# Gated linear attention with a bilinear FFN on one core: block 3's output projection in seven quarter-block products, and a new order of steps

## The chip, the cores and the metric

The kernel runs on one core of a Trainium2 chip. The metric is device time in microseconds (us): the median of several executions. The profile is of one execution; its span (first to last recorded activity) is a little shorter than that execution's own time.

Engines by the profile's names: PE (TensorE, matmuls; PEld are its weight loads), DVE (VectorE), ACT (ScalarE), POOL (GpSimd), SP (SyncE, here only an issuer of DMAs).

## What is computed

Inputs q, k, v and alpha have the shape (4 batches, 8 heads, 768 tokens, 48). Each head keeps a 48 x 48 state; the result of the attention is the FFN's input.

```python
for t in range(S):
    state = alpha[:, :, t, :, None] * state + np.einsum('bhd,bhe->bhde', k[:, :, t], v[:, :, t])
    y[:, :, t] = np.einsum('bhd,bhde->bhe', q[:, :, t], state)
x = y.transpose(0, 2, 1, 3).reshape(B * S, H * D)       # 3072 x 384
out = ((x @ w_a) * (x @ w_b)) @ w_out                   # 384 -> 1536 -> 384
```

Inputs and output are float32; the kernel multiplies in bf16.

## The kernel before, in words

**Blocks.** The 3072 tokens are worked in six blocks (`chunks` 0 to 5), two batches by 256 tokens each: 512 columns, or four groups of 128 rows. Blocks 0 and 1 hold the first 256 tokens of the four batches, 2 and 3 the next, 4 and 5 the last, so the states go from block 0 to 2 to 4 and from 1 to 3 to 5.

**Steps.** The whole kernel is a list, `PROGRAM` (line 17 on). Each entry is `block: step arguments`, and `OPS` maps a step to a function. The program is walked once, and each step puts its instructions behind those already there on its engine; every engine runs its own in that order, and the framework adds the semaphores between engines. So the order of this list sets the order of work on each engine, and a step that has to wait holds up whatever stands behind it on that engine. Engines are named by a letter: V DVE, S ACT, P POOL, Y SP.

*Attention steps.* `ld` loads one of alpha, q, k, v (POOL or SP issues it). `ln`, `l2`, `l2s`, `R`, `AQ`, `ra`, `lv`, `E`, `mk`, `mq` form the decays and put them on keys and queries; `lv` is one DVE or POOL multiplication on half a block of q or k (`level`, L610), `R` a DVE subtraction (`rest`, L581), `E` and `ra` are ACT exponentials. `dr` and `dl` bring the decay of a half block round through DRAM (SP). `T` is a DMA transpose of one batch's keys and queries (SP, L705), `Tr` its rearrangement. `v` and `vs` bring v into two layouts (ACT, DVE or POOL). `K`, `K2` are the state products on PE (L752, L765), with raw v as one operand; `k` is the state's update on DVE (L782, L783). `D` are scores on PE (L797), `M` their masking on DVE, or `Mc` an ACT copy followed by `Mm`, a masking in place on DVE (L814). `SB`, `SA`, `Y` sum the outputs on PE (L826): carried part, then inner part, the latter reading the masked scores. `X` copies the block's transposed output `xT` to SBUF.

*FFN steps.* `a f` and `b f` are one of twelve 128-row gate and up products: three matmuls of 128x512 (L881), or of 128x256 where a block is worked by batch. `as f` copies the gate half to SBUF (ACT), `pr f` multiplies (DVE, L895) into `prod`. `o m h` is half of the output projection for row group m: six matmuls of 128x384 (L903); `ot m` copies the sum out of PSUM, `st m` stores 192 KB.

*Block 4's and 5's output projections* are done otherwise. `w_out` and `prod` are cut in quarters, and seven products of quarter sums stand for the eight plain quarter products. `TW 1` to `4` (DVE, `mix_w`, L960) form mixes of the quarters of `w_out`, once; `S 1` to `4` (DVE, `mix_p`, L971, L974) form mixes of a block's quarters of `prod`, one of them in place. `P n bank` is one quarter product, 12 matmuls of 128x192 (L989), and `P+` adds onto what the bank holds. The result lies in a bank as two halves of 192 columns, for two groups of 128 rows (g = 0 and 1). `z` copies a sum from its bank (L918, L920) or adds an earlier copy to it on DVE (`c11`, `c22`, `c12`, L1001); `zs` stores one quarter of the output (L1007).

**PSUM.** There are eight banks of 512 float32 a partition; the last number of a step is its bank. `wide(i)` is bank i with the next one.

**Buffers.** `prod` has two buffers, so block 5 writes where block 3's was. The mixes live in buffers of the attention inputs: `a_t`, `k_t`, `q_t` (two each) and `la` (one).

**Order around the change.** The list is written out, by blocks of steps from several chunks: while block n is in its FFN, block n+1 is in its attention. Block 3's eight `o` stand among block 5's attention and block 4's first `a` and `b`. Then block 4's and 5's `a`, `b` follow pair by pair, with `TW` and block 4's `S` between them, then block 4's seven products, then block 5's. The last product's sum is copied from one bank in two halves: `z c21 4 S 0` (ACT, g = 0), `z c21 4 V 1` (DVE, g = 1), with one store each from ACT's and SP's queue.

Of the kernel before, what the change touches and what calls it, by code (L numbers as in the profile page):

```python
# [8 lines left out]
F32 = mybir.dt.float32  # L9
# [69 lines left out]
1: C 1 0 2; Ce 1 0 S; v 1 V; vs 1 0 S  # L79
0: o 1 0 0; o 1 1 -; ot 1 S  # L80
1: SA 0; Y 0
2: l2s 0 V
1: K2 1 1 2 1; X 0 S
0: cs 1 0 P
2: l2 0 V
1: D 1 1 6; Mc 1 1
0: o 2 1 -; ot 2 S
1: a 2 0 0; as 2 0; a 4 0 4
2: l2s 1 V
1: b 2 0 5  # L90
2: ra 1; lv 1 q P
1: vs 1 1 V
2: R 0
1: D 1 0 6; as 4 0; k 1 0 V
2: ra 0
1: SB 1 2
2: R 1
1: k 1 1 V
2: AQ 0; E 1 i; ld v * P; E 1 b
1: pr 2 0; a 10 0 4; as 10 0; a 7 0 5; M 1 0; a 1 0 6; Mm 1 1 V; b 4 0 7; pr 4 0; b 1 0 1; a 5 0 4; as 1 0; pr 1 0  # L100
2: lv 0 q P; E 0 b; dr
1: b 10 0 6; pr 10 0; a 6 0 7; as 7 0; b 7 0 1; pr 7 0; b 5 0 5; as 5 0
2: lv 1 k P
1: b 11 0 6; pr 5 0; SA 1
2: mq 0 V
1: Y 1
2: mq 1 V
1: b 6 0 1
2: mk 1 V; E 0 i
1: as 6 0; a 0 0 0; b 0 0 7; pr 6 0; a 11 0 4; X 1 S; a 2 1 5; b 3 0 2; as 0 0; pr 0 0; as 11 0; a 3 0 3; as 3 0; a 8 0 4; b 9 0 0; b 2 1 1; a 6 1 3; pr 11 0  # L110
1: as 2 1; a 9 0 5; as 9 0; pr 3 0; o 2 0 2
3: ln *; l2s 0 P; l2 0 P
0: st 0 Y
1: a 5 1 5; pr 2 1
2: lv 0 k V
1: as 8 0; a 8 1 1; as 8 1; b 8 0 6; a 3 1 7; pr 9 0; a 10 1 0
2: mk 0 V
1: pr 8 0
2: T 1
1: b 8 1 4; pr 8 1; b 5 1 1  # L120
2: dl
1: as 5 1; pr 5 1
3: l2s 1 P
1: as 6 1; b 6 1 6; pr 6 1; as 3 1; b 3 1 3; pr 3 1
2: Tr 1 S; K2 * * 4 5; k * 0 V
1: as 10 1; b 10 1 1; pr 10 1
2: k * 1 V
1: a 9 1 3; as 9 1; o 2 1 -
3: ra 1
2: v 0 S; T 0  # L130
1: b 9 1 3; pr 9 1; a 4 1 0; a 1 1 1
2: v 1 S; vs 1 0 V
1: b 11 1 4; as 1 1; a 7 1 6
4: ld a * Y
1: as 4 1
3: ld q * Y
1: b 1 1 5; pr 1 1; b 4 1 3
3: ra 0
1: pr 4 1; a 11 1 7
2: Tr 0 V; D 1 1 0; M 1 1  # L140
# [84 lines left out]
4: lv 0 k P; E 0 i; E 1 i
3: SA 0
4: mk 0 V
3: Y 0; X 0 S; Y 1
4: ld v * P; v 0 V
3: X 1 S  # L230
2: o 1 0 0; o 1 1 -
3: a 2 * 6; a 1 * 2
4: E 1 b; v 1 V; vs 0 0 V
3: a 9 * 3
2: ot 2 S
4: mk 1 V
3: b 2 * 1; as 2 *; as 9 *
4: vs 1 1 S
3: b 9 * 4; b 5 * 3; a 4 * 5
4: mq 1 V; T 0; Tr 0 S  # L240
3: pr 2 *; a 5 * 1
4: dr
3: a 11 * 6; as 11 *; a 3 * 7
5: l2 0 V
3: pr 9 *
4: T 1
3: b 11 * 4
5: l2s 1 V; R 0; R 1
3: pr 11 *; b 4 * 6
2: ot 1 S  # L250
3: as 4 *; pr 4 *; b 3 * 0
5: ra 0
3: b 1 * 4; as 3 *
5: lv 0 q P
3: pr 3 *; a 6 * 5; as 1 *; pr 1 *
4: dl; D 0 1 6; M 0 1
3: as 5 *; pr 5 *; as 6 *
5: lv 0 k V
4: K * 0 0; k * 0 V
2: st 2 Y  # L260
4: Tr 1 S
5: AQ 1
3: b 6 * 4; pr 6 *
4: vs 1 0 S
1: st 1 Y
5: E 1 i
3: a 8 * 5; as 8 *
5: ld v * P; E 0 b; mq 0 V
2: o 3 0 3; o 3 1 -
4: D 1 1 4  # L270
5: E 0 i; E 1 b; dr
2: ot 3 S
4: SB 0 0; D 0 0 6; M 0 0; Mc 1 1
3: b 8 * 2; pr 8 *
5: mk 0 V; lv 1 q V
3: a 7 * 3; as 7 *; a 0 * 4; as 0 *
5: lv 1 k V
4: Mm 1 1 V; SB 1 6
5: mk 1 V
4: vs 0 1 P; SA 0  # L280
2: st 1 Y
4: D 1 0 2; Mc 1 0; Mm 1 0 V; Y 0
3: b 7 * 4; b 0 * 5; pr 0 *
5: mq 1 V
3: a 10 * 2; as 10 *
2: st 3 Y
5: K * 0 3
4: SA 1; Y 1; X 1 S
3: o 2 0 2; b 10 * 5
4: X 0 V; a 0 * 0; a 6 * 1  # L290
5: v 0 V
3: pr 10 *; pr 7 *
5: T 0; T 1
4: a 3 * 5; b 3 * 4; as 3 *
5: dl
# [12 lines left out]
3: ot 1 V; o 3 1 -
5: D 1 1 2
4: as 6 *  # L310
5: D 0 0 0; Mc 0 0; Mc 1 1
3: ot 3 V
5: D 1 0 6; M 1 0
3: st 2 Y
4: b 6 * 4; pr 6 *
3: o 0 0 5
5: SB 0 0; vs 0 0 V; SB 1 2; D 0 1 6; M 0 1
4: a 7 * 4
5: Mm 0 0 V
3: o 0 1 -; ot 0 V  # L320
5: vs 1 0 S; Mm 1 1 V
3: st 3 Y; st 0 Y
4: a 4 * 6
5: SA 1; SA 0; vs 0 1 S; Y 0; X 0 V; vs 1 1 S; Y 1; X 1 V
3: st 1 Y
4: b 9 * 5; pr 9 *; as 7 *; b 7 * 4; pr 7 *; TW 1 V; as 4 *; b 4 * 7; pr 4 *
4: a 5 * 0; as 5 *; b 5 * 1; pr 5 *
4: TW 2 V
4: a 8 * 2; as 8 *; b 8 * 3; pr 8 *
4: TW 3 V  # L330
4: a 1 * 4; as 1 *; b 1 * 5; pr 1 *
# [12 lines left out]
5: a 9 * 6; as 9 *; b 9 * 7; pr 9 *
4: S 3 V
5: a 10 * 0; as 10 *; b 10 * 1; pr 10 *
5: a 7 * 2; as 7 *; b 7 * 3; pr 7 *
5: a 1 * 4; as 1 *; b 1 * 5; pr 1 *
5: a 0 * 6; as 0 *; b 0 * 7; pr 0 *
5: a 2 * 0; as 2 *; b 2 * 1; pr 2 *  # L350
5: a 8 * 2; as 8 *; b 8 * 3; pr 8 *
4: P 1 6; z p1 1 S; P 2 7; z c11 2 V; zs c11 Y; P+ 6 6; z u2 6 S; P 5 0; z p5 5 S
5: S 1 V
4: P+ 7 6; z c22 7 V; zs c22 Y
5: S 2 V
4: P+ 3 0; z c12 3 V; zs c12 Y; P+ 4 6
5: S 3 V; S 4 V
4: z c21 4 S; zs c21 Y
5: P 1 1; z p1 1 S; P 2 2; z c11 2 V; zs c11 Y; P+ 6 1; z u2 6 S; P 5 3; z p5 5 S; P+ 7 1; z c22 7 V; zs c22 Y; P+ 3 3; z c12 3 V; zs c12 Y; P+ 4 1; z c21 4 S 0; z c21 4 V 1; zs c21 S 0; zs c21 Y 1
"""  # L360


@with_exitstack
def kernel(
# [11 lines left out]
    nc = tc.nc  # L376
# [756 lines left out]
```

## Time and profile before

| | us |
|---|---|
| median of 3 runs | 189.93 |
| lowest, highest | 189.7, 190.2 |
| the profiled execution's own time | 189.66 |
| its span | 187.9 |
| PE busy | 180.7 |
| DVE busy | 149.1 |
| ACT busy | 119.2 |
| POOL busy | 51.7 |
| granted TensorE clock | 1.0 throughout |

Matmuls are pipelined: a row's mean duration of one matmul is longer than the distance from one to the next, so the pace is taken from pieces of the chain (a time and a count) and not from the mean. Idle time of an engine ends with a releaser, inferred from semaphores: "[0.79 <-ACT ot L918]" says that the instruction followed 0.79 us of idleness which ended with ACT's. The window rows give, after the stretch and its length, the busy time of PE, PEld, DVE, ACT and POOL with instruction counts in brackets, the granted clock, the DMA share and GB/s.

### The profile page before, as it was taken

How to read it: one execution, taken by the hardware profiler on the slowest of the kernel's cores; microseconds unless marked ns; L12 is line 12 of the kernel's file. 1: busy time of each engine (PE TensorE's matmuls, PEld its weight loads, DVE VectorE, ACT ScalarE, POOL GpSimd, SP SyncE). 2: the span in 40 equal slices, each digit the busy share in tenths (PEclk: the TensorE clock that was granted, in tenths of full speed). 3: DMA queues.
4: the chain of work that ended last, by engine and by line, in shares of the span. 5: the costliest groups of instructions: out<-in, count | busy, mean ns of one | idle time of the engine just before them, and what ended most of it. 6: DMA issues, size and time to landing. Idle time of an engine off the chain costs nothing.

```text
span 187.9 us, 6287 instructions
## 1 busy us (share of the span) xinstructions
PE 180.7 (96%) x2658; PEld 118.0 (63%) x2673; DVE 149.1 (79%) x267; ACT 119.2 (63%) x225; POOL 51.7 (28%) x74
## 2 busy tenths in 40 slices
PE   7979999999999999999999999999999999999992
PEld 3868885566788876645456645555556444448992
DVE  2587988889979799997898999997487988865641
ACT  4467685678984888796898768942567244443230
POOL 8999573995080510007100006000000000000000
PEclk9999999999999999999999999999999999999999
DMA  5999999999998999999999296989322000000233
GB/s 146 254 224 196 265 236 253 233 249 264 243 223 130 160 236 285 278 254 149 186 245 260 48 161 123 85 115 183 59 85 84 9 0 0 0 0 3 85 130 126
DMA packets 65774, 29.43 MB, mean 157 GB/s; under 512 B 55777, under 2 KB 64113, under 8 KB 65745
## 3 DMA queue, kind: packets, MB, share of 16 engines
q1 hardware_dynamic: 46976, 16.34, 40.9%
q0 software_dynamic: 18624, 12.58, 39.4%
q8 instruction: 21, 0.34, 0.7%
q10 hardware_dynamic: 144, 0.10, 0.2%
q14 instruction: 9, 0.07, 0.1%
HBM read 25.98 MB, written 4.74 MB: 164 GB/s over the span
## 4 chain that ended last, share of the span: by engine, by line
PE 86%; ACT 6%; DMA 3%; issue 2%; POOL 1%; DVE 0%; POOLq 0%
PE psum L881 47%; PE psum L903 16%; PE psum L989 7%; PE psum L826 5%; DMA v_t<-in_v_dram 3%; PE psum L797 3%; ACT vx L918 2%; PE psum L696 2%; PE psum L591 1%; ACT la L514 1%; PE psum L752 1%; PE psum L765 1%; PE psum L658 1%; PE psum L549 1%; PE psum L550 1%
## 5 line engine op out<-in xcount | busy, mean ns | idle before, releaser
L881 PE MATMUL psum<-xT,wa_t 128*128 128x512 bf16 (+1 forms) x264 | 56.5, 336 | 0.5 <-issue 0.2
L881 PE MATMUL psum<-xT,wb_t 128*128 128x512 bf16 (+1 forms) x262 | 56.0, 335 | 0.6 <-issue 0.3
L881 PEld LDWEIGHTS <-wa_t 128*128 128x128 bf16 x270 | 25.8, 98 | 19.9 <-issue 0.5
L881 PEld LDWEIGHTS <-wb_t 128*128 128x128 bf16 x270 | 25.6, 98 | 19.5 <-issue 0.3
L903 PE MATMUL psum<-wo_t,prod 128*128 128x384 bf16 x192 | 34.7, 326 | 0.0
L903 PEld LDWEIGHTS <-prod 128*128 128x128 bf16 x192 | 17.9, 98 | 11.8
L610 POOL TENSOR_TENSOR q_t<-q_t,ra 128x384 f32<-128x384 f32 x6 | 6.1, 1009 | 53.9 <-ACT ra L603 30.9
L918 ACT ACTIVATE ot<-psum 128x384 f32<-128x384 f32 (+1 forms) x20 | 9.7, 485 | 12.1 <-PE psum L989 8.0
L918 ACT ACTIVATE vx<-v_t 32x384 bf16<-32x384 bf16 x26 | 13.5, 521 | 0.5
L810 ACT ACTIVATE m<-psum 128x768 bf16<-128x768 f32 x14 | 11.0, 810 | 3.9 <-PE psum L797 3.9
L636 DVE TENSOR_TENSOR QKp<-q_t,beta 128x768 bf16<-128x768 f32 x10 | 9.5, 954 | 2.8 <-POOL q_t L610 1.7
L514 ACT ACTIVATE la<-a_t 128x1536 f32<-128x1536 f32 (+2 forms) x9 | 9.5, 1055 | 2.9 <-DMA a_t<-in_alpha_dram 2.9
L806 DVE TENSOR_TENSOR m<-psum,mask 128x768 bf16<-128x768 f32 x10 | 9.5, 953 | 0.8 <-PE psum L797 0.6
L636 DVE TENSOR_TENSOR QKp<-k_t,invb 128x768 bf16<-128x768 f32 x10 | 9.5, 954 | 0.3
L826 PE MATMUL psum<-m,vx 64*64 64x128 bf16 (+1 forms) x576 | 8.7, 205 | 0.0
L507 POOL DMA_DIRECT2D v_t<-in_v_dram x8 | 8.5, 1064 | 0.0
L989 PEld LDWEIGHTS <-prod 128*128 128x128 bf16 x96 | 8.0, 98 | 0.2
L1001 DVE TENSOR_TENSOR ot<-psum,ot 128x384 f32<-128x384 f32 x6 | 3.3, 557 | 5.9 <-PE psum L989 5.6
L826 PEld LDWEIGHTS <-vx 64*64 64x64 bf16 x576 | 7.6, 108 | 0.2
L826 PE MATMUL psum<-kqT,Sm 64*64 64x128 bf16 x144 | 7.3, 220 | 0.4 <-DVE Sm L779 0.4
L814 DVE TENSOR_TENSOR m<-m,mask 128x768 bf16<-128x768 bf16 x14 | 7.5, 551 | 0.0
L625 ACT ACTIVATE beta<-psum 128x384 f32<-128x384 f32 x10 | 4.8, 495 | 3.5 <-PE psum L596 3.4
(292 smaller groups left out, 341.2 us busy)
## 6 DMA issues: line engine op xcount, KB each, us to landing
out_dram<-ot SPq DMA_DIRECT2D x23, 192.0 KB, 2.1
q_t<-in_q_dram SPq DMA_DIRECT2D x3, 768.0 KB
k_t<-in_k_dram SPq DMA_DIRECT2D x3, 768.0 KB
a_t<-in_alpha_dram POOLq DMA_DIRECT2D x2, 768.0 KB, 12.1
v_t<-in_v_dram POOLq DMA_DIRECT2D x4, 384.0 KB, 7.5
a_t<-in_alpha_dram SPq DMA_DIRECT2D x2, 768.0 KB
a_t<-in_alpha_dram POOLq DMA_DIRECT2D x3, 384.0 KB, 8.2
k_t<-in_k_dram POOLq DMA_DIRECT2D x3, 384.0 KB, 7.1
```

What stands on the lines that cost most here:

```text
L507: eng.dma_start(out=t[:, us, hs].rearrange("p b h r d -> p (b h) (r d)"), in_=src[ch.b0 + us.start:ch.b0 + us.stop, hs, ch.s * 2 * C:(ch.s ...
L514: nc.scalar.activation(out=ch.la[:, us, hs].rearrange("p b h r d -> p (b h r d)"), in_=ch.a[:, us, hs].rearrange("p b h r d -> p (b h r d) ...
L610: eng.tensor_mul(x, x, by)
L636: eng.tensor_mul(QKp[ch.c % 2][:, u, j, :, hs, :D], src[:, u, hs].rearrange("p h r d -> p r h d"), f)
L806: nc.vector.tensor_mul(m, x, maskn())
L810: nc.scalar.activation(out=m, in_=x, func=AF.Copy)
L814: eng.tensor_mul(m, m, maskn())
L826: nc.tensor.matmul(o, lhsT=lhsT, rhs=rhs, start=(g, c) not in begun, stop=False, skip_group_check=True)
L881: nc.tensor.matmul(p, lhsT=(wa_t, wb_t)[w][:, kk, f * 128:(f + 1) * 128], rhs=ch.xT[:, kk, us, :], start=(kk == 0), stop=(kk == KT - 1))
L903: nc.tensor.matmul(op, lhsT=ch.prod[:, f, at:at + C], rhs=wo_t[:, f, :], start=(f == 0), stop=(f == NFF - 1))
L918: nc.scalar.activation(out=o_, in_=i_, func=AF.Copy)
L989: nc.tensor.matmul(o[:, g], lhsT=A[:, f, g * C:(g + 1) * C], rhs=W[:, f], start=(not more and g == 0 and f == 0), stop=(f == LH - 1), skip ...
```

## The change

Everything from the step after block 0's first `ot` (about 45.5 us into the span) is written in a new order; what stands ahead has only other line breaks.

- Block 3's eight `o`, four `ot` (three DVE, one ACT) and four `st` are replaced by `P 2`, `P 1`, `P 5`, `P+ 6`, `P+ 7`, `P+ 3`, `P+ 4` with `S 1` to `S 4` on DVE, four copies on ACT (`p1`, `p5`, `u2`, `c21`), three adds on DVE (`c11`, `c22`, `c12`) and four `zs`. They stand among block 4's and 5's `a` and `b`.
- The buffers for the mixes are taken when each is needed: `mix_w` takes `a_t` at `TW 1` and `k_t` at `TW 3`, `mix_p` takes `la` at `S 4`.
- Block 5's products 1, 6, 7, 4, which add up in one place, are now `Q`: the half g = 0 lies in bank 1, the half g = 1 in bank 2. The last `z`: DVE g = 0 with a store from SP, ACT g = 1 with a store from ACT.
- Steps of blocks 1 to 5 change places. In particular block 4's products begin among block 5's `a` and `b`, and block 5's first product comes ahead of block 4's last. Block 2's `ld v` is issued by POOL behind `lv 0 q` (before: ahead of it); `lv 1 k` of block 2, last in that group before, now comes earlier; block 5's transposes come earlier; block 4's and 5's v loads stand together.

The number of instructions stays the same for every other step.

```diff
-3: o 2 0 2; b 10 * 5
...
-3: o 1 0 0; o 1 1 -
...
-3: ot 1 V; o 3 1 -
...
+3: P 2 5
+4: a 10 * 7
+5: Mm 1 1 V
+3: S 1 V; S 2 V
...
+4: b 7 * 0; b 2 * 1; pr 4 *; a 2 * 2; as 2 *; b 8 * 3; pr 7 *; TW 2 V; a 5 * 0; as 5 *
+3: S 4 V
+4: b 10 * 2; pr 8 *; as 10 *
+3: P 1 6; z p1 1 S
+4: b 5 * 0
+5: a 11 * 3
+4: pr 2 *; TW 3 V; TW 4 V; b 11 * 1; pr 5 *
+3: P 5 7; z p5 5 S
+4: a 1 * 0
+3: P+ 6 6
+4: pr 10 *
+5: a 2 * 2
+3: S 3 V; z c11 2 V
+4: a 11 * 5
+3: z u2 6 S; P+ 7 6
...
+3: P+ 3 7
+4: as 1 *
+3: z c22 7 V
+5: b 6 * 1; a 9 * 0
+3: P+ 4 6
...
+3: z c12 3 V
```

The last stage, and block 2's steps around its v load and its `Y 1`:

```diff
-5: P 1 1; z p1 1 S; P 2 2; z c11 2 V; zs c11 Y; P+ 6 1; z u2 6 S; P 5 3; z p5 5 S; P+ 7 1; z c22 7 V; zs c22 Y; P+ 3 3; z c12 3 V; zs c12 Y; P+ 4 1; z c21 4 S 0; z c21 4 V 1; zs c21 S 0; zs c21 Y 1
+5: S 4 V; P 2 0; z p1 1 S
...
+5: z c11 2 V; zs c11 Y; Q+ 6 1; P 5 3; z u2 6 S; S 3 V; Q+ 7 1; z p5 5 S; P+ 3 3; z c22 7 V; z c12 3 V; zs c22 Y
+5: zs c12 Y; Q+ 4 1; z c21 4 S 1; zs c21 S 1; z c21 4 V 0; zs c21 Y 0
...
-2: AQ 0; E 1 i; ld v * P; E 1 b
...
+2: ra 0; lv 0 q P
...
+2: mq 0 V; ld v * P
...
+2: SB 1 0; vs 0 1 V; SB 0 2; vs 1 0 V
+1: b 11 1 6
+3: R 0
+2: Mm 0 1 V
+1: o 3 0 4; pr 11 1; o 3 1 -; ot 0 S
+3: lv 0 q V
+2: Mm 1 0 V; Y 1; Mm 0 0 V; SA 1; SA 0
```

The functions:

```diff
     def mix_w(n, eng):
-        if n == 1:
-            x, y = (late(t)[:, :2 * LH * HM].rearrange("p (w f e) -> p w f e", w=2, f=LH) for t in "ak")
-            mix.update({1: x[:, 0], 2: x[:, 1], 3: y[:, 0], 4: y[:, 1]})
+        at = (n - 1) // 2
+        if 2 * at + 1 not in mix:
+            x = late("ak"[at])[:, :2 * LH * HM].rearrange("p (w f e) -> p w f e", w=2, f=LH)
+            mix.update({2 * at + 1: x[:, 0], 2 * at + 2: x[:, 1]})
...
-    def block_mm(ch, n, i, more):
+    def block_mm(ch, n, i, more, apart=False):
...
-        o = bank(i)[:, :2 * HM].rearrange("p (g e) -> p g e", g=2)
+        o = wide(i)[:, :, :HM] if apart else bank(i)[:, :2 * HM].rearrange("p (g e) -> p g e", g=2)
...
+        "Q": lambda x, n, i: block_mm(x, int(n), i, False, True),
+        "Q+": lambda x, n, i: block_mm(x, int(n), i, True, True),
```

More of the change, by code (lines that the diff above doesn't have):

```diff
@@ L101 @@
[L101 to L116, printed above, removed]
@@ L236 @@
+4: mq 1 V
+5: ra 1
+3: a 4 * 1; a 3 * 2; as 3 *; b 3 * 3
 4: mk 1 V
[L237 to L259 removed]
@@ new lines @@
+5: lv 1 q V
+3: a 6 * 2; pr 4 *
+1: st 1 Y
+3: as 5 *; pr 5 *; as 11 *; as 1 *; b 11 * 3; a 2 * 4
+4: vs 0 1 P
+3: b 2 * 6
+5: AQ 0
+3: as 2 *
+4: K * 0 7
+3: pr 11 *
+4: D 0 1 4
+3: as 6 *
+5: E 0 i; E 0 b
+4: vs 0 0 V
+3: a 0 * 2; pr 2 *
+4: Tr 1 S
+3: b 6 * 3; b 1 * 0
+4: M 0 1
+5: mk 0 V
+4: k * 0 V
+5: E 1 b; E 1 i
+2: o 3 0 4
+5: dr
+4: vs 1 1 S
+2: o 3 1 -; ot 3 S
+5: lv 0 q P
+4: D 1 1 5
+3: pr 1 *
+4: D 0 0 0
+3: b 8 * 7
+5: mq 0 V
+3: a 8 * 4; pr 6 *
+4: Mc 1 1
+3: as 8 *
+4: Mm 1 1 V; SB 0 5
```

486 lines of the change are left out of this document (260 added, 226 removed).

## The prediction

> **What bounds the kernel now.** I read the page first, then what TensorE (PE) waits for, then the chain of waits, then the last microseconds of the timeline.
>
> ```profile
> span 187.9 us, 6287 instructions
> PE 180.7 (96%) x2658; PEld 118.0 (63%) x2673; DVE 149.1 (79%) x267; ACT 119.2 (63%) x225; POOL 51.7 (28%) x74
> PEclk9999999999999999999999999999999999999999
> ```
>
> ```profile
> PE psum L532 <- DVE og L432: 1.2, 1, 1.2
> PE psum L797 <- ACT bl L679: 0.6, 1, 0.6
> PE psum L881 <- issue: 0.5, 3, 0.2
> PE psum L826 <- DVE Sm L779: 0.4, 1, 0.4
> PE psum L549 <- ACT la L514: 0.4, 1, 0.4
> ```
>
> PE is busy in 96% of the span at full clock. Its listed waits are 3.1 us (us in total, times, longest); the four behind other engines belong to lines that first run in the first 20 us, which the change leaves alone. So PE's own work is the time, and an edit pays if it shortens that work, or the tail behind it, without making PE wait.
>
> ```profile
> 127.87 1.08 PE psum L903 x6
> ...
> 132.19 2.92 PE psum L903 x18
> ...
> 156.20 10.74 PE psum L881 x49
> ...
> 170.61 13.87 PE psum L989 x168
> ```
>
> These pieces of the chain are PE running back to back. L903 is the plain output projection (`o`): 2.92 us for three steps, 0.973 a step of 6. L989 is the quarter product (`P`): 13.87/14 = 0.991 us for 12 matmuls, 82.6 ns each. The `o` at 127.87 stands ahead of 64x64 attention work and costs 1.08: 0.10 us for turning into that work. No row isolates the way back; I take the same.
>
> ```profile
> 184.51 0.33 ACT L918 ACTIVATE ot<-psum 128x192 f32<-128x192 f32 x1 [2.43 <-PE psum L989]
> 184.87 0.37 ACTq L1007 DMA_DIRECT2D out_dram<-ot  x1
> 184.87 0.36 DVE L920 COPY ot<-psum 128x192 f32<-128x192 f32 x1 [0.79 <-ACT ot L918]
> 185.26 0.34 SPq L1007 DMA_DIRECT2D out_dram<-ot  x1
> ```
>
> At the end the two halves of the last sum leave one bank one after the other: DVE's copy waits for ACT's, and its store is issued 0.39 us after ACT's.
>
> **The change part by part.** *Products (PE).* Removed: 8 `o`, 8 x 0.973 = 7.78 us. Added: 7 products, 7 x 0.991 = 6.94. Sum **-0.84**. A product holds PE for 0.99 us beside any neighbour, so standing among gate and up steps changes nothing here.
>
> A rule of the Trainium skill speaks against this term: "TensorE: Matmul & The Clock Gate", "Back-to-back issue gap", has sustained weight-load-and-matmul pairs at 81 ns for 128 columns and 131 for 512. An estimate on the straight line between them is 89 ns for 192 and 114 for 384, so 84 x 89 - 48 x 114 = +2.0 us. This case's trace disagrees: 82.6 ns and 2.92/18 = 162 ns, and 10.74/49 = 219 for 128x512.
>
> *Order on PE.* The new order leaves the full-array steps for 64x64 work 28 times instead of 27, counted in the program. One more way in and out: **+0.20**.
>
> *Last sum.* In two banks, the DVE half needs only its own six matmuls, which end 6 x 0.083 = 0.5 us before PE does. So its 0.36 us copy and SP's issue are over when ACT's copy ends; the last store is then ACT's, issued 0.39 us before the store that is last now. **-0.36**, a little kept back for the shared queue.
>
> *Added DVE and ACT work.*
>
> ```profile
> L974 DVE TENSOR_TENSOR q_t<-q_t,prod 128x1536 bf16<-128x1536 bf16 x2 | 1.9, 946 | 0.0
> L1001 DVE TENSOR_TENSOR ot<-psum,ot 128x384 f32<-128x384 f32 x6 | 3.3, 557 | 5.9 <-PE psum L989 5.6 <-issue 0.3
> L920 DVE COPY ot<-psum 128x384 f32<-128x384 f32 x4 | 2.2, 556 | 0.8 <-PE psum L903 0.7
> L918 ACT ACTIVATE ot<-psum 128x384 f32<-128x384 f32 x19 | 9.4, 493 | 9.6 <-PE psum L989 5.6 <-DVE ot L1001 2.5 <-PE psum L903 1.5
> ```
>
> ```profile
> 130.00:145.00 15.00, 14.79 (x268) 8.66 (x270) 9.87 (x19) 9.21 (x16) 0.00 (x0) 1.00 0.34 78
> 145.00:158.00 13.00, 12.79 (x82) 5.97 (x73) 11.56 (x18) 4.78 (x8) 0.00 (x0) 1.00 0.06 20
> 158.00:170.60 12.60, 12.55 (x60) 5.77 (x60) 9.49 (x14) 5.97 (x10) 0.00 (x0) 1.00 0.00 1
> ```
>
> DVE gains 4 mixes of 0.946 and 3 adds of 0.557 and loses 3 copies of 0.556: +3.8 us. ACT gains 4 copies for 1: +1.5. By my placing of the new order (steps end to end at the row durations) they fall at 137 to 159 us. The third number after the stretch's length is DVE: 30.9 of 40.6 us. With the addition it is 34.7, 85%, and each mix stands at least one gate or up step ahead of the product that reads it. Cost **0** while that room hides it; uncovered, a mix costs its 0.95. The stores go from 4 of 192 KB to 4 of the same size, and SP issues them in a stretch where DMA is at most 0.34 busy: 0. The lazily taken buffers add no instruction: 0. The four weight mixes keep their length; the first moves ahead to about 129, which relieves the fullest stretch, 145 to 158.
>
> *Reordered steps of blocks 1 to 4.* No row shows a wait that this could remove, so it can only cost. I laid each engine's queue end to end against PE's due times and looked at the thinnest places. Two are late or on the edge.
>
> First, block 2's `Y 1` (due 76.3 us). Behind the copy of block 1's last gate half, DVE has to do in this order a half product, two copies `vs`, `R 0`, a mask product, a half product, block 3's `lv 0 q` and the mask product that `Y 1` reads.
>
> ```profile
> 68.50 0.51 DVE L920 COPY vx<-v_t 32x384 bf16<-32x384 bf16 x2
> ...
> 71.09 0.43 DVE L895 TENSOR_TENSOR prod<-as__1541,psum 128x256 bf16<-128x256 bf16 x1
> 71.42 0.95 DVE L581 TENSOR_TENSOR lh<-l 128x768 f32<-128x768 f32 x1
> ...
> 75.72 0.55 DVE L814 TENSOR_TENSOR m<-m,mask 128x768 bf16<-128x768 bf16 x1
> ```
>
> ```profile
> 123.71 0.55 DVE L610 TENSOR_TENSOR q_t<-q_t,ra 128x384 f32<-128x384 f32 x1
> 124.18 0.55 DVE L610 TENSOR_TENSOR k_t<-k_t,a_t 128x384 f32<-128x384 f32 x1
> ```
>
> ```profile
> 72.00:79.00 7.00, 7.00 (x226) 4.78 (x215) 6.71 (x16) 5.84 (x11) 0.00 (x0) 1.00 1.19 280
> ```
>
> Start to start, a half product is 0.33 (71.09 to 71.42) and an 0.55 operation 0.47 (123.71 to 124.18). So 0.33 + 2 x 0.51 + 0.9 + 0.47 + 0.33 + 0.47 + 0.55 = 4.1 us, begun about 0.5 us after the gate half ends at 71.9: done at 76.5, and 0.1 to 0.2 for the hand-over. Late by 0.15 to 0.35; I take **0.25**. The window says the same of the place: DVE already works 6.71 of 7.00 us there. Behind `Y 1` on PE stand both `SA`, `Y 0` and block 3's sums, and all wait.
>
> Second, block 2's v load, which the state product `K2` reads raw. GpSimd (POOL) now issues it behind `lv 0 q`, and that waits for an exponential late in ACT's queue.
>
> ```profile
> 51.77 1.00 POOL L610 TENSOR_TENSOR q_t<-q_t,ra 128x384 f32<-128x384 f32 x1 [6.74 <-ACT ra L603]
> 52.73 1.19 POOL L507 DMA_DIRECT2D v_t<-in_v_dram  x1
> ```
>
> ```profile
> 64.79 0.63 PE psum L765 x64
> ```
>
> ```profile
> DMA to landing us min/median/max: 5.5/7.5/13.3
> ```
>
> Now it is issued at 52.7, a dozen us ahead of `K2` at 64.8. In the new order ACT reaches the exponential at about 56.4, POOL is through at 57.5, and `K2` is due at 63.8, about 6.3 us later. At the smallest landing, 5.5 us, it is free; at the median, 7.5, it costs 1.2. The range is 0 to 1.2. I take **0.15**, nearest the smallest: no other load is queued by POOL in those microseconds, while several of the eight that make the median were issued in the first stage, behind the weights. In block 4 and 5 POOL issues both v loads together, tens of us ahead of use: 0.
>
> Of SP's queue the loads, decay rows and transposes keep their sequence, and the stores of finished rows move between them.
>
> ```profile
> kqT<-QKp SPq DMA_TRANSPOSE x8, 5.6
> ```
>
> The thinnest is block 3's second transpose, which I place at 90 us: with 5.6 to landing it is there at 95.6, and DVE takes it up at about 96. Cost 0; each us later would cost one. What lies after 130 us has the quiet DMA of the windows above.
>
> *Sum.* -0.84 + 0.20 - 0.36 + 0.25 + 0.15 = **-0.60 us**. Against the profiled execution: 189.66 - 0.60 = 189.06. The median shown is 189.93, 0.27 above it, so I forecast **189.3**.
>
> **The rivals.** *No stall* (both thin places hold): -0.84 + 0.20 - 0.36 = -1.00, so 188.9. For it: my two places are late by less than a hand-over. Against: DVE's 96% in that window.
>
> *v lands at the median.* `K2` waits 1.2 us instead of 0.15: +0.45, so 190.4. For it: the move itself. Against: the quiet queue.
>
> *The last sum gains nothing*, because DVE's half still waits for PE's last matmul or the store queue holds it: -0.24, so 189.7. Against it: separate banks and a wait written for its own matmuls.
>
> *Block 3's q load is late (slower).* DVE's `lv 0 q` stands in front of the mask product of `Y 1`, and DVE reaches it at 75.6 us.
>
> ```profile
> 65.75 2.60 SPq L507 DMA_DIRECT2D q_t<-in_q_dram  x1
> ```
>
> ```profile
> 77.13 0.55 DVE L610 TENSOR_TENSOR q_t<-q_t,ra 128x384 f32<-128x384 f32 x1
> ```
>
> SP issues it at 65.75 now and DVE uses it at 77.13 without a gap, so it landed within 11.4 us; no tighter bound is shown. In the new order SP issues it behind the second transpose, 0.4 us later. If it takes the whole 11.4 it lands at 77.5 and costs 1.9: +1.3, so 191.2. It costs from a landing after 75.6, 9.5 us behind its issue, and turns the change slower than before from 10.1 us. For it: the DMA share of that window is over 1, full. Against it: 280 GB/s there would move the 1.5 MB of this and the load ahead in under 6 us.
>
> *The small products pay their weight load.* If a product among other steps went at the pace of a weight load,
>
> ```profile
> L989 PEld LDWEIGHTS <-prod 128*128 128x128 bf16 x96 | 8.0, 98 | 0.2
> ```
>
> 98 ns for 82.6, 84 of them cost 8.2 us for the 7.78 removed: +1.3 on the sum, 190.6, slower. Against it: 168 in 13.87 us with a load for each.
>
> By the rule of the Trainium skill quoted above, the same term would be +2.0 for -0.84, the time 192.1; the 14 products in the trace speak against it.
>
> **How the numbers follow.** About 0.3% (0.57 us) is what a measurement of this kernel can tell from no change. Chances: forecast (-0.85 to -0.35) 0.42, of which 0.23 beyond 0.57; no stall 0.18; v at the median 0.15, of which 0.04 slower by over 0.57; last sum without gain 0.07; q late 0.16, of which 0.13 slower; weight load 0.02. Faster 0.23 + 0.18 = **0.41**, slower 0.04 + 0.13 + 0.02 = **0.19**, within 0.3% **0.40**. The range starts at the no-stall end with 0.1 for the spread of its terms, **188.8**, and ends at **190.7**, above the late v and the weight load; beyond it lie the upper half of the late q and little else, about 0.1.
>
> **What would show it.** PE's busy time 0.6 to 0.8 us smaller; `P` in 0.99 us pieces among gate and up steps; in the list of PE's waits a DVE mask product before the `Y` of 76 us with 0.15 to 0.35, and possibly a v load before `K2` at 64; the last DVE copy over before ACT's begins, and the span ending about 2.9 us after the last matmul. PE waiting for a mix (DVE, at 145 to 158 us) or for `as` copies would make it wrong, and so would a `q_t` load as releaser of DVE at 75 us.

## The result, and the profile after

The changed kernel takes 192.39 us (median of 6 runs, 191.95 to 192.74) where the kernel before takes 189.88 (6 runs): 1.22% slower, ratio 1.0122, 95% interval 1.0097 to 1.0147. The profiled execution took 192.55 us with a span of 190.8; that of before 189.66 with 187.9. In some runs of the experiments the TensorE clock was granted at 0.83 on average from 10 to 20 us, which makes them about 2 us longer; where the profile of such a run is used below, the text says that PE came late.

The page of the changed kernel, first the span and the busy times:

```profile
span 190.8 us, 6336 instructions
PE 180.9 (95%) x2692; PEld 120.5 (63%) x2709; DVE 155.0 (81%) x271; ACT 120.6 (63%) x228; POOL 53.2 (28%) x74
```

DVE was to gain 3.8 us and gained 5.9. What PE waited for (us in total, times, longest us):

```profile
PE psum L828 <- DMA v_t<-in_v_dram: 1.2, 1, 1.2
...
PE psum L944 <- issue: 0.8, 5, 0.2
PE psum L889 <- issue: 0.5, 1, 0.5
...
PE psum L944 <- DVE m L869: 0.4, 1, 0.4
PE psum L944 <- DVE Sm L842: 0.3, 1, 0.3
```

These waits are new: the v load at `K2`, gate and up steps (L944) waiting for DVE, and 0.5 us in the output sums (L889) that has no releaser. (The short "issue" waits of gate and up steps are not new; they were 0.5 us before.) In PE's timeline of the changed kernel they stand at these places:

```profile
51.65 0.49 PE L944 MATMUL psum<-xT,wb_t 128*128 128x256 bf16 x3 [0.34 <-DVE Sm L842]
54.79 0.49 PE L944 MATMUL psum<-xT,wa_t 128*128 128x256 bf16 x3 [0.35 <-DVE m L869]
66.61 0.69 PE L828 MATMUL psum<-v_t,QKp 64*64 64x48 bf16 x64 [1.20 <-DMA v_t<-in_v_dram]
```

```profile
106.70 0.57 PE L889 MATMUL psum<-m,vx 64*64 64x64 bf16 x36 [0.52 <-issue]
```

The list leaves out the short waits. A finer reading: from 45.5 us on I put PE's steps end to end, each with the duration of its kind (0.648 us for a gate step, 0.976 for `o`, 0.990 for `P` and so on), and take the difference to when each step began. In the kernel before, this lag is 0.1 us at the end. In the changed kernel it comes in four places:

| lag of PE in us at | before | after |
|---|---|---|
| 57 us, block 1's `a 5` | -0.05 | 1.52 |
| block 2's `K2` | -0.03 | 2.80 |
| behind block 2's `Y 1` | 0.0 | 3.09 |
| behind block 3's `Y 0` | 0.11 | 3.79 |
| the last product | 0.13 | 3.85 |

The steps themselves add up to 183.50 us in the new order and 184.18 in the old, so 0.68 less; the lag is 3.72 more; the rest, the stretch behind PE's last matmul, is 0.2 less. That gives +2.8; the two profiled executions differ by 2.9. From 107 us to the end, where the seven products, their mixes and their copies stand, the lag grows by 0.06.

The chain of waits of the changed kernel, around block 3's and block 4's products:

```profile
149.63 0.99 PE psum L1055 x12
150.62 1.94 PE psum L944 x9
152.57 0.99 PE psum L1055 x12
...
176.51 11.07 PE psum L1055 x132
```

A product among gate and up steps takes 0.99 us, as one among products. And the end:

```profile
187.11 0.36 DVE L983 COPY ot<-psum 128x192 f32<-128x192 f32 x1
187.60 0.33 ACT L981 ACTIVATE ot<-psum 128x192 f32<-128x192 f32 x1 [2.48 <-PE psum L1055]
187.96 0.37 ACTq L1073 DMA_DIRECT2D out_dram<-ot  x1
```

DVE's copy is over before ACT's begins, as intended. From the start of ACT's copy to the end of the span it is 190.8 - 187.60 = 3.2 us, before 187.9 - 184.51 = 3.4.

Where does the first 1.5 us come from? DVE between 49 and 53 us, then POOL from 49 to 60 us, in the changed kernel:

```profile
49.31 1.15 DVE L794 COPY vx<-v_t 128x768 bf16<-128x768 bf16 x1
50.38 0.94 DVE L644 TENSOR_TENSOR ll<-lh 128x768 f32<-128x768 f32 x1
51.25 0.34 DVE L842 TENSOR_TENSOR Sm<-psum,bl 128x192 bf16<-128x192 f32 x1
51.70 0.36 DVE L845 TENSOR_TENSOR tmp<-psum,Sm 128x192 f32<-128x192 f32 x1
52.09 0.98 DVE L846 TENSOR_TENSOR S<-tmp,bl 128x192 bf16<-128x192 f32 x1
```

```profile
49.03 1.22 POOL L673 TENSOR_TENSOR q_t<-q_t,ra 128x384 f32<-128x384 f32 x1 [4.48 <-DMA q_t<-in_q_dram]
51.85 1.00 POOL L673 TENSOR_TENSOR k_t<-k_t,a_t 128x384 f32<-128x384 f32 x1 [1.61 <-DMA k_t<-in_k_dram]
58.47 1.00 POOL L673 TENSOR_TENSOR q_t<-q_t,ra 128x384 f32<-128x384 f32 x1 [5.18 <-ACT ra L666]
59.41 1.19 POOL L570 DMA_DIRECT2D v_t<-in_v_dram  x1
```

The same DVE operations in the kernel before, and the masking that stood beside POOL's first multiplication (51.77) there:

```profile
45.77 0.35 DVE L731 COPY vx<-v_t 128x768 bf16<-128x768 bf16 x1
...
51.04 0.36 DVE L783 TENSOR_TENSOR S<-tmp,bl 128x192 bf16<-128x192 f32 x1
...
51.79 0.95 DVE L806 TENSOR_TENSOR m<-psum,mask 128x768 bf16<-128x768 f32 x1
```

The copy of v took 0.35 us in the kernel before and takes 1.15 here; it ends 0.2 us after POOL's multiplication. The update `S<-tmp,bl` takes 0.98 for 0.36 and ends 0.2 us after POOL's second one. Between them `Sm<-psum,bl`, with no POOL operation beside it, and `tmp<-psum,Sm`, which reads one operand from PSUM and ends 0.2 us into POOL's second one, have their usual length. So the first theory was: **an operation of POOL and one of DVE on SBUF data hold each other up**, and the queue behind is late. Its rival: DVE is late because its first operation here now waits 0.80 us for block 2's logarithm (to 46.70 us), which hangs on a load. For the second place the theory is the load alone: issued at 59.41, landed at 66.47, 7.06 us.

### The profile page after: what moved, and what is told of

It is laid out like the page before. It is cut to its first block, busy times and chain, and to the rows that moved or that the text cites. A ratio compares the mean times of both kernels' runs of the same rounds, so it can differ in the third digit from the quotient of the medians.

```text
span 190.8 us, 6336 instructions
## 1 busy us (share of the span) xinstructions
PE 180.9 (95%) x2692; PEld 120.5 (63%) x2709; DVE 155.0 (81%) x271; ACT 120.6 (63%) x228; POOL 53.2 (28%) x74
## 4 chain that ended last, share of the span: by engine, by line
PE 63%; DMA 16%; POOL 9%; DVE 5%; issue 3%; ACT 1%; POOLq 0%; ACTq 0%
PE psum L944 37%; PE psum L1055 11%; DMA q_t<-in_q_dram 7%; PE psum L966 6%; DMA a_t<-in_alpha_dram 6%; PE psum L889 4%; DMA v_t<-in_v_dram 4%; PE psum L860 2%; POOL wb_t L550 2%; POOL a_t L570 1%; PE psum L654 1%; POOL wa_t L550 1%; POOL v_t L570 1%; DVE m L877 1%; ACT la L577 1%
## 5 line engine op out<-in xcount | busy, mean ns | idle before, releaser
L944 PE MATMUL psum<-xT,wa_t 128*128 128x512 bf16 (+1 forms) x261 | 55.9, 335 | 1.4 <-DMA wa_t<-in_moe_w_a_dram 0.5
L944 PE MATMUL psum<-xT,wb_t 128*128 128x512 bf16 (+1 forms) x263 | 55.7, 335 | 1.1 <-issue 0.5
L944 PEld LDWEIGHTS <-wb_t 128*128 128x128 bf16 x270 | 25.7, 98 | 19.4 <-issue 0.8
L944 PEld LDWEIGHTS <-wa_t 128*128 128x128 bf16 x270 | 25.4, 98 | 19.0 <-issue 0.7
L966 PE MATMUL psum<-wo_t,prod 128*128 128x384 bf16 x144 | 26.3, 327 | 0.0
L981 ACT ACTIVATE ot<-psum 128x384 f32<-128x384 f32 (+1 forms) x23 | 11.0, 481 | 17.2 <-PE psum L1055 16.1
L966 PEld LDWEIGHTS <-prod 128*128 128x128 bf16 x144 | 13.3, 98 | 8.7 <-issue 0.3
L1055 PEld LDWEIGHTS <-prod 128*128 128x128 bf16 x144 | 12.1, 98 | 1.4
L699 DVE TENSOR_TENSOR QKp<-q_t,beta 128x768 bf16<-128x768 f32 x10 | 10.3, 1030 | 1.7 <-POOL q_t L673 1.7
L889 PE MATMUL psum<-m,vx 64*64 64x64 bf16 (+1 forms) x576 | 9.0, 205 | 0.6 <-issue 0.5
L1067 DVE TENSOR_TENSOR ot<-psum,ot 128x384 f32<-128x384 f32 x9 | 5.0, 553 | 4.2 <-PE psum L1055 4.1
L889 PEld LDWEIGHTS <-vx 64*64 64x64 bf16 x576 | 7.6, 108 | 1.1 <-issue 1.1
L889 PE MATMUL psum<-kqT,Sm 64*64 64x128 bf16 x144 | 7.5, 220 | 0.3 <-DVE Sm L842 0.3
L634 POOL TENSOR_TENSOR l<-la 64x384 f32<-64x384 f32 x3 | 3.0, 986 | 17.2 <-PE psum L654 13.5
## 6 DMA issues: line engine op xcount, KB each, us to landing
v_t<-in_v_dram POOLq DMA_DIRECT2D x4, 384.0 KB, 11.4
```

Source lines behind the costliest of these rows:

```text
L699: eng.tensor_mul(QKp[ch.c % 2][:, u, j, :, hs, :D], src[:, u, hs].rearrange("p h r d -> p r h d"), f)
L889: nc.tensor.matmul(o, lhsT=lhsT, rhs=rhs, start=(g, c) not in begun, stop=False, skip_group_check=True)
L944: nc.tensor.matmul(p, lhsT=(wa_t, wb_t)[w][:, kk, f * 128:(f + 1) * 128], rhs=ch.xT[:, kk, us, :], start=(kk == 0), stop=(kk == KT - 1))
L966: nc.tensor.matmul(op, lhsT=ch.prod[:, f, at:at + C], rhs=wo_t[:, f, :], start=(f == 0), stop=(f == NFF - 1))
L981: nc.scalar.activation(out=o_, in_=i_, func=AF.Copy)
L1055: nc.tensor.matmul(o[:, g], lhsT=A[:, f, g * C:(g + 1) * C], rhs=W[:, f], start=(not more and (apart or g == 0) and f == 0), stop=(f == LH ...
```

## Experiments

**One cause at a time, on the changed kernel.** `e2_v_early` moves one step:

```diff
 1: vs 1 1 V
+2: ld v * P
 ...
 2: mq 0 V
-2: ld v * P
```

> The changed kernel with one step moved: block 2's v load stands on POOL ahead of block 2's lv 0 q, right behind the copy vs 1 1 that frees its buffer. In the changed kernel it was issued at 59.41 and PE waited 1.20 us for it at K2 (to 66.61). Theory: the load is issued at about 55.5, lands by 63, K2 waits for nothing, and the time falls by the 1.2 us to 191.1 to 191.4. Rival: DVE is full from there to 80 us, so the 1.2 us is lost again at Y 1, and the time stays at 192.4.

Measured: 192.10 us (4 runs), ratio 1.0081 (1.0055 to 1.0108); the changed kernel had 1.0122 (1.0097 to 1.0147), so a gain is not clear of noise. PE no longer waits at `K2`: its row has no idle time. But the next DMA was not there either. DVE of this kernel:

```profile
65.75 0.55 DVE L838 TENSOR_TENSOR tmp<-psum,S 128x384 f32<-128x384 f32 x1
68.28 0.56 DVE L839 TENSOR_TENSOR Sm<-tmp,bl 128x384 bf16<-128x384 f32 x1 [1.99 <-DMA bl<-row]
```

The state's update waited 1.99 us for the decay that comes through DRAM. PE lost 0.92 us to it at 69.56, and about 1.7 us in all between `K2` and the end of `Y 1`, where the changed kernel loses 0.3. So the rival, with all of it lost again, is nearer than the theory: the wait for v is gone, and most of what it cost is given back behind a second transfer.

`e3_pool_late` moves three steps, so that POOL's multiplications start later:

```diff
 2: l2 0 V; l2s 0 V
-2: ra 1
 2: l2s 1 V; R 0
-2: lv 1 q P; lv 1 k P
 ...
 0: ot 2 S
+2: ra 1; lv 1 q P; lv 1 k P
```

> The changed kernel with block 2's exponential ra 1 and POOL's multiplications lv 1 q and lv 1 k put behind block 0's ot 2 on ACT, some 3 us later, everything else as it is. Theory: two DVE operations were held up by POOL multiplications that ran at the same time (the copy of v at 49.31 took 1.15 us for 0.35, the state update at 52.09 took 0.98 for two of 0.36); moved away, the copy takes 0.35 again, PE's loss of 1.6 us between 48 and 57 us falls to about 0.8, and the time to 191.5 to 191.9. Rival: DVE's queue was late because it waits for block 2's logarithm (first operation behind it at 46.70); then the copy may shorten, but the loss and the time stay, 192.2 to 192.5.

Measured: 192.51 us (6 runs, 191.37 to 194.18), ratio 1.0106 (1.0055 to 1.0157): inconclusive by time. In its profile PE came 2 us late already at 46 us and could lose less to DVE, so a second profile of the same kernel was taken:

> The same kernel as e3_pool_late, for one profile at full clock. Theory (POOL and DVE hold each other up): PE's loss between 48 and 57 us is 0.2 to 0.9 us instead of 1.6, the copy of v 0.35. Rival (late logarithm): 1.3 to 1.6.

Measured: 191.54 us in one run, inside the spread of the six above, so the time still settles nothing and the trace has to. PE's lag at 57 us is 0.35 instead of 1.52. DVE, in this repeat:

```profile
46.13 0.56 DVE L579 TENSOR_TENSOR l<-la 128x384 f32<-128x384 f32 x1 [0.35 <-ACT la L571]
...
48.73 0.35 DVE L788 COPY vx<-v_t 128x768 bf16<-128x768 bf16 x1
...
50.72 0.36 DVE L840 TENSOR_TENSOR S<-tmp,bl 128x192 bf16<-128x192 f32 x1
...
52.77 1.23 DVE L977 COPY vx<-v_t 32x384 bf16<-32x384 bf16 x2
```

DVE still waits for the logarithm, with the same steps in the same order, and the copy and the update are short. The two small copies at 52.77 take 1.23 for 0.51: POOL's multiplications now run at 51.90 and 52.87. The stretching went along with POOL, as the theory has it.

The logarithm itself came 0.57 us earlier in this execution (46.13 for 46.70), so the gain in lag is not POOL's alone. The two can be told apart on DVE: from its first operation behind the logarithm to the masking in place it needs 6.29 us in the changed kernel (46.70 to 52.99) and 4.86 here (46.13 to 50.99), 1.43 less, which is what the two stretched operations had too much. An estimate of what that is worth on PE: in the changed kernel that masking began 7.49 us behind PE's transposes (45.50) and PE's lag at 57 us was 1.5; in `e2_v_early`, with the same two operations stretched but PE later and no wait for the logarithm, it began 6.40 us behind them and the lag was about 0.4. So lag and lateness of DVE go us for us, and without the 1.43 the changed kernel would have lost about 0.1 there even with its late logarithm.

`e5_v_first` takes the copy out of POOL's way instead:

```diff
+1: v 1 V
 2: l2 0 V; l2s 0 V; ra 1; l2s 1 V; R 0; lv 1 q P; lv 1 k P
 1: C 1 0 0
-1: v 1 V
```

> The changed kernel with one step moved: block 1's copy of v on DVE stands ahead of block 2's l2 0 again, as in the kernel before, so DVE does it in the 0.8 us in which it waited for the logarithm. Theory: it takes 0.35 us there, beside no POOL operation, and 1.1 us is gone from the DVE queue that PE waited for at 51.65, 53.95 and 54.79; the loss up to 57 us falls from 1.6 to about 0.5 and the time to 191.3 to 191.6. If only the order counts and not POOL beside it, the queue gets 0.35 shorter and the time is 192.0 to 192.2.

Measured: 192.67 us (4 runs, 192.31 to 194.98), ratio 1.0141 (1.0077 to 1.0204): no gain. The copy takes 0.35, and other DVE operations stand beside POOL in its place:

```profile
49.22 1.83 DVE L628 TENSOR_TENSOR l<-la 64x384 f32<-64x384 f32 x2
51.08 0.96 DVE L638 TENSOR_TENSOR lh<-l 128x768 f32<-128x768 f32 x1
52.07 1.67 DVE L638 TENSOR_TENSOR ll<-lh 128x768 f32<-128x768 f32 x1
```

1.83 for 1.12 and 1.67 for 0.95. The expectation was wrong in assuming that the hold-up belonged to the copy; it falls on whatever DVE does on SBUF data at that moment. PE came 2.6 us late in this profile too, so its lag of 0.75 at 58 us isn't to be compared.

`e15_both` joins the two moves.

> The changed kernel with both moves: block 2's v load behind vs 1 1, and block 2's ra 1, lv 1 q, lv 1 k behind block 0's ot 2. Theory: each gives what it gave alone, about 0.9 us at K2 and 0.7 to 1.2 us by 57 us, so 190.4 to 191.0 where before is 189.9 (ratio 1.003 to 1.006). Rival: both are the same lateness and don't add, ratio 1.008 or more.

Measured: 191.68 us (4 runs), ratio 1.0086 (1.0058 to 1.0113): no better than the v load alone (1.0081), as the rival said. In its profile the lag is 0.33 at 57 us and at `K2`, and then 1.2 us are lost behind `K2`, where DVE waits 1.44 us for the decay (`bl<-row`), and at `Y 1`. A load that is earlier doesn't help when the one behind it isn't. What the move of POOL gave here the profile doesn't show: PE stood 0.6 us later at 46 us than in the changed kernel, as it did in `e2_v_early`, where the lag at 57 us is about 0.4 with POOL unmoved.

**The suspected cause alone, on the kernel before.** `e12_pool_early`:

```diff
 2: l2 0 V
+2: ra 1; lv 1 q P
 1: D 1 1 6; Mc 1 1
 ...
-2: ra 1; lv 1 q P
```

> The kernel before with one thing of the change alone: block 2's exponential ra 1 and POOL's multiplication lv 1 q stand ahead, as in the changed kernel, so that POOL runs at about 49 to 50 us beside DVE's subtractions R 0 and R 1 instead of at 51.77 beside a masking that reads PSUM. Theory (POOL and DVE hold each other up on SBUF data): one of the DVE operations of 0.95 us takes up to 1.9, POOL's takes more than 1.0, and PE loses 0 to 0.8 us near 51 us (ratio 1.000 to 1.004). Rival (POOL beside DVE costs nothing): all keep their length, ratio 1.000.

Measured: 191.00 us (6 runs) for 189.70, ratio 1.0059 (1.0043 to 1.0074): this one move costs about 1.1 us in a kernel that is otherwise as before, more than expected. DVE and POOL of this kernel:

```profile
51.07 0.77 DVE L768 TENSOR_TENSOR S<-tmp,bl 128x192 bf16<-128x192 f32 x1
...
52.96 2.21 DVE L799 TENSOR_TENSOR m<-m,mask 128x768 bf16<-128x768 bf16 x1
```

```profile
50.45 1.18 POOL L595 TENSOR_TENSOR q_t<-q_t,ra 128x384 f32<-128x384 f32 x1 [5.43 <-ACT ra L588]
51.58 1.19 POOL L492 DMA_DIRECT2D v_t<-in_v_dram  x1
52.78 1.01 POOL L595 TENSOR_TENSOR q_t<-q_t,ra 128x384 f32<-128x384 f32 x1
53.74 1.00 POOL L595 TENSOR_TENSOR k_t<-k_t,a_t 128x384 f32<-128x384 f32 x1
```

The masking in place, 0.55 us elsewhere, began 0.18 us behind the start of a POOL multiplication and ended 0.4 us behind the end of the next one: it waited for both. The masking ahead of it (52.09, 0.95 us, which reads PSUM) was not held up. PE lost 0.85 us to it at 55.58:

```profile
55.58 0.49 PE L866 MATMUL psum<-xT,wa_t 128*128 128x256 bf16 x3 [0.68 <-DVE prod L880]
```

The operations that were stretched are not the subtractions that the expectation named. In the kernel before, every POOL operation behind 45 us that reads SBUF ran beside DVE operations that read one operand from PSUM, but for 0.1 us at 52.7; its order had kept the two apart.

**Parts of the order.** The last sum alone, `e1_banks`: the kernel before with `Q 1 1`, `Q+ 6 1`, `Q+ 7 1`, `Q+ 4 1` and the two halves as in the change (block 5's `P 2` goes to bank 0).

> The kernel before with one part of the change alone: block 5's products 1, 6, 7 and 4 add up in two banks, and the last sum leaves them by DVE (g = 0, store from SP) and ACT (g = 1, store from ACT). Theory: DVE's copy no longer waits for ACT's, the last store is issued 0.39 us earlier, and the time falls by 0.2 to 0.4 us (ratio 0.998 to 0.999). Rival: nothing, because the end of the span hangs on something else than that store (ratio 1.000).

Measured: 189.68 us (12 runs) for 190.04 (29 runs), ratio 0.9976 (0.9954 to 0.9998). In the profile the end behind ACT's copy is 187.6 - 184.43 = 3.2 us for 3.4; the trace shows 0.2 of it, the interval holds 0.04 to 0.9.

`e8_after128` has the changed order up to block 4's first gate steps, then the old one with eight `o`.

> The other half: the order of the changed kernel up to 128 us, then that of the kernel before, with block 3's eight plain projections and the last sum in one bank. Theory: it has all the loss and none of the gain: 3.2 to 3.8 us slower than before (ratio 1.017 to 1.020). Rival: the loss belongs to the products behind 128 us; then ratio 1.005 or less.

Measured: 194.21 us (4 runs), ratio 1.0225 (1.0197 to 1.0253). The lag repeats at the same places (1.53 at 57 us, 2.79 at `K2`, 3.09, 3.75) and 0.9 us come at the seam of the two orders. So the loss is there without any of the products; the seam makes it more than was expected.

`e4_before128` is the reverse. In it block 5's state product is overwritten in its bank before it is read, so that its output is not the reference's; its instructions are those of the parts it joins.

> The order of the kernel before up to block 4's first gate steps (about 128 us), from there the order of the changed kernel: block 3's seven products in place of its eight plain projections, and the last sum in two banks. Theory: all of the loss lies in the reordered steps ahead of 128 us (3.8 us on PE by 107 us), and what comes behind is worth -0.8 for the products, +0.1 to +0.2 for turns and -0.2 to -0.4 for the end: 0.7 to 1.1 us faster than before (ratio 0.994 to 0.9965). Rival: the products or DVE's mixes for them cost what they bring; then no faster than the two banks alone, ratio 0.998 or more.

Measured: 190.94 us (12 runs), ratio 1.0066 (1.0038 to 1.0093): slower, against the theory. The lag is 0.11 us to the seam and grows to 1.8 within 6 us behind it, where PE waits 0.6 us for DVE's copy of `xT` and 0.3 for an ACT copy: the two orders don't fit together there. It says nothing on the products, whose effect the seam hides.

`e6_before98`, with the seam at 98 us, has a like flaw in one row group of block 2: its `o 0` is overwritten before its copy.

> As the kernel with the order of before up to 128 us, but only up to 98 us (block 2's o 0), so that the changed order of 98 to 128 us is in it: block 3's outputs, block 4's decays, and the POOL operations beside DVE at 111 to 114 us. Theory: that stretch costs the 0.5 to 0.7 us that PE stood still at 106 us in the changed kernel and nothing else: ratio 0.997 to 1.001. Rival: that stop came from the lateness of DVE ahead of 98 us; then no loss, ratio 0.994 to 0.9965.

Measured: 190.37 us (12 runs), ratio 1.0024 (0.9998 to 1.0051). The lag is 0.13 at the seam and behind block 3's `Y 0`: the stop of 106 us is gone, which is what the rival said, though not for which reason. The lag grows by 0.7 near 113 us, where DVE is beside POOL again, so the ratio is not the rival's. Next come the same kernel with `o 0` in another bank (`e9_before98b`), and that kernel with POOL's work near 113 us given to ACT and DVE (`e10_before98_nopool`):

```diff
-4: vs 0 1 P
+4: vs 0 1 S
 ...
-5: lv 0 q P
+5: lv 0 q V
```

> The order of the kernel before up to 98 us (block 2's o 0, whose bank is now 7), the changed order behind it, with the seven products and the two banks. It is the kernel e6_before98 with one bank corrected: there o 0 was overwritten before its copy, so that row group of block 2 was wrong, with the same instructions. Theory: as that one, PE loses about 0.6 us near 113 us, where DVE is late because POOL's two copies and its multiplication run beside it (109.37: 1.75 us for 0.95), and the time is 0 to 0.3% from before (ratio 0.998 to 1.003).

> As e9_before98b, but block 4's copies vs 0 1 are on ACT and block 5's multiplication lv 0 q on DVE instead of POOL. Theory (an operation of POOL and one of DVE on SBUF data hold each other up): DVE does 0.55 us more and is still earlier by about 0.7, since 1.75 goes back to 0.95 and 0.66 to 0.35; the loss near 113 us falls below 0.2, and the time to 0.3 to 0.5% below before (ratio 0.995 to 0.997), faster than both kernels. Rival (DVE is late there for its own amount of work): DVE has more to do and the loss grows, ratio 1.000 or more.

Measured: 191.81 us (5 runs), ratio 1.0123 (1.0103 to 1.0142), and 190.50 (8 runs), ratio 1.0051 (1.0029 to 1.0072). Neither ratio is the one expected, since the new bank of `o 0` made PE wait 1.4 us for an ACT copy in both. The second is 0.7% faster than the first, with intervals that don't meet; 0.1 to 0.8% had been expected between them. DVE of the first and of the second at the same steps (ll, copy of v, query product):

```profile
109.20 1.07 DVE L627 TENSOR_TENSOR ll<-lh 128x768 f32<-128x768 f32 x1
110.19 0.66 DVE L777 COPY vx<-v_t 128x768 bf16<-128x768 bf16 x1
110.78 1.75 DVE L682 TENSOR_TENSOR QKp<-q_t,beta 128x768 bf16<-128x768 f32 x1
```

```profile
108.97 0.96 DVE L627 TENSOR_TENSOR ll<-lh 128x768 f32<-128x768 f32 x1
109.85 0.35 DVE L777 COPY vx<-v_t 128x768 bf16<-128x768 bf16 x1
110.12 0.95 DVE L682 TENSOR_TENSOR QKp<-q_t,beta 128x768 bf16<-128x768 f32 x1
```

DVE has one operation more and is earlier. PE's lag near 113 us grows by 0.1 instead of 0.7. So the theory has it, and DVE's own amount of work was not the cause.

`e13_best` keeps `o 0` in its old bank with the copy right behind it:

> As e10_before98_nopool (order of before up to 98 us, then the changed order with the seven products and two banks, block 4's vs 0 1 on ACT and block 5's lv 0 q on DVE), but block 2's o 0 stays in bank 0 and its copy ot 0 follows at once, as in the kernel before, so that PE doesn't wait for bank 7. Theory: PE loses no more than 0.3 us anywhere, and products, turns and end are worth -0.84 + 0.20 - 0.36: 0.7 to 1.0 us faster than before (ratio 0.9945 to 0.9965). Rival (the products' mixes or their copies cost too): ratio 0.998 or more.

Measured: 189.53 us (12 runs) for 189.96 (17 runs), ratio 0.9976 (0.9961 to 0.9990): faster than the kernel before by 0.4 us and than the changed one by about 2.8, but by less than the 0.7 to 1.0 expected. The lag is 0.66: 0.47 arises at the seam (PE waits 0.24 for ACT's `ot` and then for a bank), the rest elsewhere. Of the 0.68 that the products save on PE it gives back 0.53, so it is as fast as the two banks alone. By time, then, no run shows a gain of the products; the 0.68 is read from PE's steps.

**The stop at 106 us.** `e11_o_between` puts block 2's `o 1` between block 3's `Y 0` and `SA 1`.

> The changed kernel with block 2's o 1 (12 matmuls of 128x384) between block 3's Y 0 and SA 1, where five groups of small products stood in one piece. In the changed kernel PE stood still for 0.52 us in the middle of Y 0 (106.17 to 106.70) with no engine or DMA as releaser, and so in each kernel with that order. Theory: PE ran out of fetched instructions in the long run of small products; o 1 behind Y 0 doesn't shorten what comes ahead of the stop, so it stays in Y 0 or moves, with 0.2 to 0.7 us left: 191.9 to 192.5. Rival (Y 0 waits for something that DVE or ACT does): then o 1 behind it leaves it exactly as it is, 0.5 at the same instruction, 192.4.

Measured: 194.35 us (4 runs), ratio 1.0246: slower, because the bank of `o 1` was now waited for (1.6 us for ACT's copy of `xT`), which neither side had. The stop stays 0.5 us in `Y 0`, as both sides allowed. It is there, 0.5 to 0.7 us with no releaser and behind the same matmul of `Y 0`, in all eight profiles with the changed order ahead of it and in none of the four with the order of before up to 98 us, although the steps from 98 us on are nearly the same. In each of the eight, PE goes on 2.3 to 2.6 us after a 16 KB packet of the instruction queue q8 began (104.37 and 106.70 in the changed kernel). That speaks for a fetch of instructions, but at 129.76 a like packet stands beside PE work that is as dense, without such a stop. Whether it is a fetch or a dependency that the trace doesn't show stays open.

## Why the prediction was wrong

*Products, 7 x 0.991 for 8 x 0.973, and the turns, +0.20:* right. Steps end to end give -0.68 where -0.64 was forecast; 0.99 holds among gate and up steps. The rival of the weight loads falls. So does the pace that the Trainium skill, "TensorE: Matmul & The Clock Gate", "Back-to-back issue gap", gives; that its sum, 192.1, lies near the measured 192.39 is chance, since the products cost nothing like it.

*Last sum, -0.36:* right in kind, too large: 0.2 by the profiles. DVE's copy is out of the way and the last store is issued earlier, as said. But the span now ends 2.8 us after ACT begins to issue that store (190.8 - 187.96, and 187.6 - 184.79 in `e1_banks`), where it ended 2.6 us after SP began to issue the last one before (187.9 - 185.26); the sum took the two to be alike.

*Added DVE and ACT work, 0:* right. From 133 us to the end the lag grows by 0.02, and PE waits for no mix.

*Block 2's `Y 1`, 0.25:* right, 0.29. PE's list of waits has no row for it; it shows inside `Y 1`, where no matmul begins between 79.35 and 79.60 while DVE's mask product ends at 79.55.

*Block 2's v load, 0.15:* wrong in size. I took it near the smallest landing, 5.5 us, with 6.3 us free; it took 7.06, which makes about 0.8, and was issued about 0.4 us later against PE than I had placed it (59.41, with PE 1.5 us late, for 57.5). Together it cost 1.28. The reason given, a quiet queue, was no row of that stretch. The rival, v at the median, had the size (1.2), partly by luck: it knew nothing of the later issue.

*"Reordered steps ... it can only cost ... Two are late or on the edge":* this step failed, and the largest part of the loss is here. The thin places were looked for with each operation's usual length on its own engine, and what POOL costs DVE was put at nothing. The new order puts block 2's `lv 1 q` and `lv 1 k` on POOL 2.7 and 3.1 us ahead of where they were, beside DVE operations on SBUF data, and the later of the two waits for the other. PE's lag at 57 us is 1.5, where I had 0. That POOL is the cause is shown by the traces of the runs that move it (e14: the stretching moves with it) and by time in two pairs of kernels: moved in the kernel before (e12: +1.1 us), and taken off POOL near 113 us (e9 to e10: -0.7%). In the changed kernel itself moving POOL made no difference in time that is clear of noise; the share of the late logarithm in the 1.5 is an estimate, about 0.1. The Trainium skill, "SBUF — State Buffer", "SBUF: two separate sides", says this: the port pair that DVE and GpSimd share is an exclusive lock, held for the whole instruction, which a DVE operation needs in a two-port fast mode or, against a GpSimd operation that reads SBUF, with two SBUF inputs. The traces agree: a copy goes from 0.35 to 1.15 us, a masking in place from 0.55 to 2.21 and a product from 0.95 to 1.75, and the masking that reads PSUM keeps its length. In the kernel before no DVE operation behind 45 us is stretched in this way, so no row showed the price; that POOL's steps had moved against DVE's could be read from the order.

*The stop at 106 us, 0.70:* not foreseen, cause open.

*Block 3's q load:* DVE did not wait for it; that rival fell.

In sum -0.60 was forecast and the profiled executions show +2.9. The difference of 3.5 is 1.5 by 57 us (by the estimate nearly all from POOL beside DVE), 1.1 from the v load beyond what was taken, 0.7 from the stop and 0.2 from the end.

## What to carry to other kernels

When steps change places, look at pairs of engines and not at one queue after the other: here a POOL operation that reads SBUF cost DVE up to its whole length unless DVE was then reading from PSUM, and moving a 1 us multiplication ahead by 1.3 us (`e12_pool_early`) cost 1.1 us of a PE-bound kernel. A load that is made to wait behind compute is better priced at its median landing than at its smallest, and the next transfer behind it too. A gain of 0.6 us is only there if the order around it loses nothing: here the two banks alone, with no reordering, were worth as much as the best version with the products.

## What the runs showed of the hardware

- An operation of DVE on SBUF data and one of POOL that reads SBUF held each other up in these traces: the one that began later is recorded as running until 0.2 to 0.4 us behind the end of the other, in place of its usual length. A DVE operation of 0.55 us waited for two POOL operations in a row (2.21 us). It goes both ways: POOL's two copies of v, 1.04 us in the kernel before, beside a masking that reads PSUM, take 2.29 in the changed kernel, beside DVE's subtractions. The two rows are from the kernel before and the changed one:

```profile
116.36 1.04 POOL L920 COPY vx<-v_t 32x384 bf16<-32x384 bf16 x2
```

```profile
109.60 2.29 POOL L983 COPY vx<-v_t 32x384 bf16<-32x384 bf16 x2 [11.65 <-DVE vx L794]
```

- The four 384 KB loads of v by POOL landed 5.5 to 13.1 us behind their issue in the kernel before, with a median of 7.5, and 7.1 to 14.7 us in the changed one, with a median of 11.4. The last number of each row is the median, before and after:

```profile
v_t<-in_v_dram POOLq DMA_DIRECT2D x4, 384.0 KB, 7.5
```

```profile
v_t<-in_v_dram POOLq DMA_DIRECT2D x4, 384.0 KB, 11.4
```
